# Retention and soft mixture of experts in one kernel: where block copies of y run, and which key tiles are loaded twice

## The chip, the cores and the metric

One core of a Trainium2 chip runs the whole kernel. The metric is device time in microseconds, from one launch; the times shown are medians over runs of the same program. Engines by their names in the profile: PE is TensorE's matmul side and PEld its weight loads, DVE is VectorE, ACT is ScalarE, POOL is GpSimd, SP is SyncE, which issues every DMA of this kernel.

## The reference

Two stages. The first is retention over 4 batches, 8 heads, 768 tokens, head size 64, with a decay `gamma` per head:

```
state = gamma * state + k_t (outer) v_t
y_t   = q_t @ state / sqrt(D)
```

The second takes y as x, 3072 tokens by 512, through a soft mixture of 8 experts with 4 slots each. All in float32:

```
logits = x @ phi                          # 3072 x 32
slot_input = softmax over tokens (logits).T @ x
slot_out[e] = relu(slot_input[e] @ w1[e]) @ w2[e]
out = softmax over slots (logits) @ slot_out
```

## The kernel before, in words

The tokens of a sequence are cut into chunks of 128, and one chunk of one batch is a step: 24 steps, two of them a pair, 12 pairs. The loop `for P in range(NPP)` (L505) makes one pass for each pair, numbered from 0 here as in the code: "pass 9" is the tenth. The order of all instructions on every engine is the order of the program text (`manual_schedule`, L96). Each pass does, for its pair:

- loads: `load_pair(P + 3)` (L229, for the last two pairs L223) and most times two weight blocks of 2 MB (`load_two`, L176). SyncE issues them in order and waits at each for its buffer; three buffers hold input pairs.
- GpSimd decays q and v of the next pair (L240, L245) and keeps the decay factors `qtab` going (L249).
- TensorE adds what the carried state gives (L280) and the values, scores times v (L289); ScalarE and VectorE copy the result out as y (L308, L309; in the last pass L305, L306). TensorE forms the state's increment from natural keys (L318), and VectorE adds it (L327).
- Keys come transposed from memory. Natural keys, needed at L318, are made by `turn_k`: four TensorE transposes (L234) and a ScalarE copy (L235), for the steps in `TURNED`. For the others (5, 7 and 9) a second, natural copy of the keys is loaded behind the pair's other inputs.
- y of a pair has to be turned to token order (`xn`) for the slot inputs. Either TensorE transposes it (`natural_mm`, L334) and ScalarE copies it out (`natural_copy`, L341); or, for the pairs in `MOVED`, one pass later VectorE turns all 32x32 blocks in place (`block_turn`, L345) into a tile `xb`, and 16 copies of 32 partitions by 256 elements put the blocks into order (`block_moves`, L355). `MOVES` says in which pass the copies run, in two parts of eight, and by which engine: a letter each, "s" for ScalarE, "g" for GpSimd, `MIX` five and three. 
- In every second pass the logits of four steps (L372), their exponentials on ScalarE (L395, L398, after VectorE's L402), and the slot sums of the four steps before (L428) follow. `combine_b` has one GpSimd operation (L474).
- At the end of a pass TensorE takes the scores of the next pair's two steps (L256), and VectorE masks them (L264) into a tile `A`.

Tiles `A`, y, `xb` and `xn` come from one ring of nine slots (`slot()`): a new tile takes a slot that has come back, and its first writer waits until that slot's last readers are done.

Behind the loop come the last slot inputs, the first expert layer (L671), the second (L757), taken in three blocks of output columns, and the combination (L733), whose pieces are copied out (L741) and stored (L744).

The constants that the change touches, L47 to L52:

```
TURNED = (0, 1, 2, 3, 4, 6, 8, 10, 11, 12, 13, 14, 15, 16, 17, 18, 19)
MOVED = (0, 2, 3, 4, 5, 6, 7, 8)
MIX = "sgssgssg"
MOVES = {1: [(0, 0, MIX)], 2: [(0, 1, MIX)], 9: [(8, 0, "s")], 10: [(8, 1, "g")]}
MOVES.update({P: [(P - 1, 0, MIX), (P - 1, 1, MIX)] for P in range(3, 9)})
```

The order in a pass, with lines left out:

```
        attend_copy(P)
        if P - 1 in MOVED:
            block_turn(P - 1)
...
        if P not in MOVED:
            natural_mm(P)
            natural_copy(P)
        for m in MOVES[P]:
            block_moves(*m)
```

Of the kernel before, what the change touches and what calls it, by code (L numbers as in the profile page):

```python
# [43 lines left out]
NIN = 3  # L44
NRING = 9
PACE = (0, 1, 0, 1, 1, 1, 1, 1, 1, 0, 1, 0)
TURNED = (0, 1, 2, 3, 4, 6, 8, 10, 11, 12, 13, 14, 15, 16, 17, 18, 19)  # L47
SIW = 48
MOVED = (0, 2, 3, 4, 5, 6, 7, 8)
MIX = "sgssgssg"  # L50
MOVES = {1: [(0, 0, MIX)], 2: [(0, 1, MIX)], 9: [(8, 0, "s")], 10: [(8, 1, "g")]}
MOVES.update({P: [(P - 1, 0, MIX), (P - 1, 1, MIX)] for P in range(3, 9)})  # L52
WITHK = [[i for i in (2 * P, 2 * P + 1) if i not in TURNED and i < NSTEP - B] for P in range(NPP)]
ROWS = [[P for P in range(1, NPP - B // 2) if len(WITHK[P]) == n] for n in range(3)]
KINDS = [n for n in range(3) if ROWS[n]]
# [31 lines left out]
def retention_soft_moe_kernel(  # L87
# [143 lines left out]
    def turn_k(i, name):  # L231
        kp = bank(name)
        for g in range(NPAIR):
            nc.tensor.transpose(kp[:, g * 128:(g + 1) * 128], st[i]["kT"][:, g, :], ident)  # L234
        nc.scalar.copy(st[i]["kn"], kp.rearrange("p (h d) -> p h d", d=D))  # L235
# [85 lines left out]
    def state_add(P):  # L321
        for k in range(2):
            d = sst[(2 * P + k) % B]
            if P < B // 2:
                nc.scalar.copy(d, pr[P]["S"][:, k])
            else:
                nc.vector.tensor_tensor(d, d, pr[P]["S"][:, k], ALU.add)  # L327

    def natural_mm(P, ks=(0, 1), names=("A2", "A3")):
        X = pr[P].setdefault("X", {})  # L330
        for k in ks:
            X[k] = bank(names[k])
            for g in range(NPAIR):
                nc.tensor.transpose(X[k][:, g * 128:(g + 1) * 128], pr[P]["yT"][:, k, g, :], ident)  # L334

    def natural_copy(P, engines=("scalar", "scalar"), ks=(0, 1)):
        if "xn" not in pr[P]:
            pr[P]["xn"] = slot()
        for k in ks:
            xn = st[2 * P + k]["xn"] = pr[P]["xn"][:, k * 512:(k + 1) * 512]  # L340
            (nc.scalar.copy if engines[k] == "scalar" else nc.vector.tensor_copy)(xn, pr[P]["X"][k])  # L341

    def block_turn(P):
        x = pr[P]["xb"] = slot()
        nc.vector.transpose(x, pr[P]["yT"].rearrange("p i g t -> p (i g t)"))  # L345

    def block_moves(P, part, on="sg"):
        if part == 0:
            xn = pr[P]["xn"] = slot()
            for k in range(2):  # L350
                st[2 * P + k]["xn"] = xn[:, k * 512:(k + 1) * 512]
        x = pr[P]["xb"].rearrange("p (m b d) -> p m b d", b=4, d=32)
        xn = pr[P]["xn"].rearrange("p (m a d) -> p m a d", a=4, d=32)
        for n, (a, b) in enumerate((a, b) for a in (2 * part, 2 * part + 1) for b in range(4)):
            {"s": nc.scalar.copy, "g": nc.gpsimd.tensor_copy}[on[n % len(on)]](xn[32 * b:32 * b + 32, :, a], x[32 * a:32 * a + 32, :, b])  # L355
# [149 lines left out]
    for P in range(NPP):  # L505
# [50 lines left out]
        if P < NPP - B // 2:  # L556
            state_mm(P)
            state_add(P)
        if P - 1 in MOVED:
            block_turn(P - 1)  # L560
        for k in range(2):
            if 2 * P + 2 + k in TURNED:
                turn_k(2 * P + 2 + k, ("A2", "Y0")[k] if P % 2 == 0 else f"A{k}")
        if P == NPP - 2:
            for m in MOVES[P]:
                block_moves(*m)
# [9 lines left out]
            continue  # L576
# [5 lines that stand above are left out]
# [255 lines left out]
```

## Time and profile before

| | us |
|---|---|
| median of 3 runs | 150.73 (150.56 to 150.92) |
| the profiled execution | 150.77 |
| its span, first to last instruction | 149.1 |
| PE busy | 138.0 (93%) |
| DVE busy | 89.2 (60%) |
| ACT busy | 70.1 (47%) |
| POOL busy | 68.1 (46%) |
| DMA moved | 60.06 MB, mean 403 GB/s |

Times of rows are microseconds from the span's start. A matmul of this kernel shows as two records. Busy time of PE counts overlapping matmuls once.

### The profile page before, as it was taken

Reading aid. Unit: us, or ns where it says so; the run is one execution under the profiler, and the core shown is the slowest. Engines: PE = TensorE matmul, PEld = TensorE weight load, DVE = VectorE, ACT = ScalarE, POOL = GpSimd, SP = SyncE. Lnnn points to the kernel's source line nnn. Section 1 sums busy time; section 2 is a strip of 40 time slices with the busy share of each in tenths; the row PEclk is TensorE's granted clock in tenths of the full one; section 3 lists DMA queues with packets and bytes.
Section 4 is the critical chain, followed back from the end, with each engine's and each line's share of the span. In section 5 each row is a group of like instructions: output and inputs, shape, how many; then the busy total and the mean of one; then the engine's idle time right before and its main releaser. Section 6 shows DMA issues by size and latency. Waiting matters only on the chain.

```text
span 149.1 us, 5532 instructions
## 1 busy us (share of the span) xinstructions
PE 138.0 (93%) x2382; PEld 102.3 (69%) x2382; DVE 89.2 (60%) x195; ACT 70.1 (47%) x172; POOL 68.1 (46%) x121
## 2 busy tenths in 40 slices
PE   7999999989999999999999999599999999999820
PEld 2778989877999799979996888465333365656600
DVE  0497837776887997799886883457510101564450
ACT  3123472737779766988587823141510000352240
POOL 1172497986969796796592989210200000000000
PEclk9999999999999999999999999999999999999997
DMA  4999999999999999999999999999999999799696
GB/s 138 408 446 411 445 428 426 420 400 440 425 425 418 398 442 414 439 402 435 420 431 418 431 418 426 415 425 404 403 442 422 422 426 431 308 400 411 276 383 247
DMA packets 6937, 60.06 MB, mean 403 GB/s; under 512 B 768, under 2 KB 768, under 8 KB 3712
## 3 DMA queue, kind: packets, MB, share of 16 engines
q1 hardware_dynamic: 6912, 59.70, 96.2%
q8 instruction: 19, 0.31, 0.8%
q14 instruction: 6, 0.05, 0.1%
HBM read 53.41 MB, written 6.29 MB: 400 GB/s over the span
## 4 chain that ended last, share of the span: by engine, by line
PE 61%; DMA 23%; POOL 6%; DVE 4%; issue 1%; SPq 1%; DVEq 0%; POOLq 0%
DMA b<-in_x_dram 10%; DMA b<-in_xw_dram 10%; PE A L757 10%; PE Y L289 8%; PE A L256 8%; PE Y L671 5%; PE A L671 5%; PE S L318 5%; PE Y L280 3%; DMA r<-in_head_dram 3%; PE sm L372 3%; PE A L234 2%; POOL r L355 2%; POOL b L245 2%; PE sm L733 2%; DVE b L741 2%
## 5 line engine op out<-in xcount | busy, mean ns | idle before, releaser
L264 DVE TENSOR_TENSOR r<-A,mi 128x512 f32<-128x512 f32 (+1 forms) x50 | 30.2, 662 | 16.3 <-PE A L256 13.4
L355 ACT COPY r<-r 32x256 f32<-32x256 f32 x78 | 31.4, 402 | 3.1 <-DVE r L345 2.2
L256 PE MATMUL A<-b 64*128 64x128 f32 x384 | 25.5, 280 | 0.3 <-DMA b<-in_kq_dram 0.3
L256 PEld LDWEIGHTS A<-b 64*128 64x128 f32 x384 | 22.7, 187 | 3.3 <-issue 1.8
L245 POOL TENSOR_TENSOR b<-b,kt 128x512 f32<-128x512 f32 x23 | 23.8, 1054 | 0.9 <-DMA b<-in_x_dram 0.9
L355 POOL COPY r<-r 32x256 f32<-32x256 f32 x50 | 19.8, 395 | 6.9 <-PE S L428 2.8
L289 PE MATMUL Y<-r,b 128*64 128x128 f32 x352 | 22.2, 277 | 0.3 <-POOL b L245 0.3
L289 PEld LDWEIGHTS Y<-r,b 128*64 128x64 f32 x352 | 19.2, 137 | 2.6 <-issue 1.2
L240 POOL TENSOR_TENSOR b<-b,qtab 128x256 f32<-128x256 f32 x20 | 14.3, 735 | 13.0 <-DMA b<-in_x_dram 9.2
L757 PE MATMUL A<-b,r 128*32 128x128 f32 (+1 forms) x352 | 14.4, 304 | 0.1
L757 PEld LDWEIGHTS A<-b,r 128*32 128x32 f32 x352 | 9.6, 109 | 6.2 <-issue 3.8
L741 ACT COPY b<-A 128x384 f32<-128x384 f32 x10 | 4.5, 483 | 17.0 <-PE A L733 15.3
L318 PE MATMUL S<-b 128*64 128x64 f32 x304 | 10.7, 222 | 0.0
L280 PE MATMUL Y<-b,sst 64*64 64x128 f32 x304 | 10.6, 276 | 0.0
L318 PEld LDWEIGHTS S<-b 128*64 128x64 f32 x304 | 10.3, 138 | 0.0
L345 DVE STREAM_TRANSPOSE r<-r 128x1024 f32<-128x1024 f32 x8 | 9.9, 1238 | 0.0
L280 PEld LDWEIGHTS Y<-b,sst 64*64 64x64 f32 x304 | 8.2, 132 | 1.2
L309 DVE TENSOR_TENSOR r<-Y,qtab 128x512 f32<-128x512 f32 x9 | 6.2, 692 | 4.6 <-PE Y L289 4.6
L235 ACT COPY b<-A 128x512 f32<-128x512 f32 x11 | 6.3, 588 | 5.7 <-PE A L234 2.3
L372 PEld LDWEIGHTS sm<-r,kt 128*32 128x32 f32 x192 | 5.4, 110 | 2.6 <-issue 2.4
L327 DVE TENSOR_TENSOR sst<-sst,S 128x256 f32<-128x256 f32 x16 | 6.0, 418 | 1.9 <-PE S L318 1.9
L671 PE MATMUL A<-b,qtab 128*32 128x512 f32 x64 | 7.1, 594 | 0.0
(160 smaller groups left out, 194.3 us busy)
## 6 DMA issues: line engine op xcount, KB each, us to landing
b<-in_wtwo_dram SPq DMA_DIRECT2D x12, 2048.0 KB, 17.2
b<-in_x_dram SPq DMA_DIRECT2D x5, 1536.0 KB, 12.7
b<-in_x_dram SPq DMA_DIRECT2D x3, 1792.0 KB, 11.1
b<-in_xw_dram SPq DMA_DIRECT2D x2, 2048.0 KB, 16.1
out_dram<-b SPq DMA_DIRECT2D x5, 768.0 KB, 5.6
b<-in_wl_dram SPq DMA_DIRECT2D x2, 1536.0 KB, 11.8
r<-in_whalf_dram SPq DMA_DIRECT2D x5, 512.0 KB, 12.3
out_dram<-b SPq DMA_DIRECT2D x6, 384.0 KB, 3.3
```

Of the source, the lines that this page charges most:

```text
L240: nc.gpsimd.tensor_tensor(q[:, 0:2], q[:, 0:2], qtab[:, 0:2], ALU.mult)
L245: nc.gpsimd.tensor_tensor(v, v, vsc[:, i // B, a:b].unsqueeze(2).broadcast_to([128, b - a, D]), ALU.mult)
L256: nc.tensor.matmul(s["sc"][r][:, g, :], s["kT"][half(r), g, :], s["qT"][half(r), g, :], start=True, stop=True, skip_group_check=True)
L264: nc.vector.tensor_tensor(s["A"][:, r, g:g + n], s["sc"][r][:, g:g + n], mask.unsqueeze(1).broadcast_to([128, n, C]), ALU.mult)
L280: nc.tensor.matmul(p["y"][k][b][half(half_of(r, g)), gl, :], sst[(2 * P + k) % B][half(r), g, :], s["qT"][half(r), g, :], start=(gl == 0 a ...
L289: nc.tensor.matmul(pr[P]["y"][k][g // 2][half(half_of(r, g)), g % 2, :], s["v"][:, 2 * g + r, :], s["A"][:, r, g, :], start=(P < B // 2 an ...
L318: nc.tensor.matmul(S_[half(r), k, g, :], s["kn"][:, 2 * g + r, :], s["v"][:, 2 * g + r, :], start=True, stop=True, skip_group_check=True)
L345: nc.vector.transpose(x, pr[P]["yT"].rearrange("p i g t -> p (i g t)"))
L355: {"s": nc.scalar.copy, "g": nc.gpsimd.tensor_copy}[on[n % len(on)]](xn[32 * b:32 * b + 32, :, a], x[32 * a:32 * a + 32, :, b])
L372: nc.tensor.matmul(q["ltp"][32 * j:32 * j + 32, :], phis[:, p, :], st[GRP * g + j]["yT"][:, p, :], start=(p == 0), stop=(p == NPAIR - 1), ...
L671: nc.tensor.matmul(hp[hf][32 * j:32 * j + 32, :], si0[:, a:a + NSLOT], w1t[hf, g, k][j], start=(g == 0 and k == 0), stop=(g == 1 and k == ...
L757: nc.tensor.matmul(op[32 * j:32 * j + 32, :w], hT[fc // 4][:, fc % 4, 4 * g + j, :], w2t[4 * g + j, cb, fc], start=(n == 0), stop=(n == le ...
```

## The change

Pair 1's y goes by block turn and copies in pass 2 instead of TensorE's transposes in pass 1, so pair 0's sixteen copies all run in pass 1. Pair 7's copies in pass 8 alternate between the two engines. Pair 8's copies all run in pass 9, fourteen on ScalarE and two on GpSimd, and pass 10 has none. Steps 7 and 9 get their natural keys by `turn_k`, in passes 2 and 3, and the loads of pairs 3 and 4 no longer hold them.

```diff
-TURNED = (0, 1, 2, 3, 4, 6, 8, 10, 11, 12, 13, 14, 15, 16, 17, 18, 19)
+TURNED = (0, 1, 2, 3, 4, 6, 7, 8, 9, 10, 11, 12, 13, 14, 15, 16, 17, 18, 19)
 SIW = 48
-MOVED = (0, 2, 3, 4, 5, 6, 7, 8)
+MOVED = (0, 1, 2, 3, 4, 5, 6, 7, 8)
 MIX = "sgssgssg"
-MOVES = {1: [(0, 0, MIX)], 2: [(0, 1, MIX)], 9: [(8, 0, "s")], 10: [(8, 1, "g")]}
-MOVES.update({P: [(P - 1, 0, MIX), (P - 1, 1, MIX)] for P in range(3, 9)})
+MOVES = {1: [(0, 0, MIX), (0, 1, MIX)], 2: [(1, 0, MIX), (1, 1, MIX)], 8: [(7, 0, "sg"), (7, 1, "sg")], 9: [(8, 0, "s"), (8, 1, "sssg")], 10: []}
+MOVES.update({P: [(P - 1, 0, MIX), (P - 1, 1, MIX)] for P in range(3, 8)})
```

## Rows read from the trace of the kernel before

**Rows 1.** Windows: busy us (instructions) by engine, PE clock, DMA share, GB/s

```profile
core 0: us, PE busy (x) PEld busy (x) DVE busy (x) ACT busy (x) POOL busy (x), PEclk, DMA share, GB/s
...
30.00:60.00 30.00, 29.58 (x584) 26.17 (x580) 24.73 (x53) 21.35 (x54) 24.25 (x42) 1.00 1.01 422
60.00:90.00 30.00, 29.64 (x581) 25.72 (x578) 25.28 (x54) 22.20 (x57) 21.79 (x38) 1.00 1.01 424
...
127.00:131.00 4.00, 4.00 (x84) 2.27 (x80) 2.14 (x5) 1.72 (x4) 0.00 (x0) 1.00 0.71 300
...
138.00:142.00 4.00, 3.59 (x70) 2.33 (x63) 1.62 (x5) 0.93 (x3) 0.00 (x0) 1.00 0.71 284
```

**Rows 2.** Chain of waits, 73 to 97 us: start, length, what

```profile
72.99 14.28 DMA b<-in_xw_dram
...
96.37 0.44 PE S L289 x7
```

**Rows 3.** Timeline, 88 to 104 us: start, length, engine, line, operation [idle before, releaser]

```profile
90.49 1.16 PE L256 MATMUL A<-b 64*128 64x128 f32 x16
...
90.88 3.46 POOL L355 COPY r<-r 32x256 f32<-32x256 f32 x8
...
92.62 1.09 PE L289 MATMUL Y<-r,b 128*64 128x128 f32 x16
...
94.38 1.29 DVE L264 TENSOR_TENSOR r<-A,mi 128x512 f32<-128x512 f32 x2 [2.89 <-POOL r L355]
...
95.12 0.43 PE L289 MATMUL A<-r,b 128*64 128x128 f32 x2 [1.41 <-DVE r L264]
```

**Rows 4.** Timeline, 81 to 89 us

```profile
81.90 3.31 ACT L355 COPY r<-r 32x256 f32<-32x256 f32 x8
...
82.36 1.43 POOL L240 TENSOR_TENSOR b<-b,qtab 128x256 f32<-128x256 f32 x2 [3.03 <-DMA b<-in_xw_dram]
...
83.15 1.86 PEld L256 LDWEIGHTS A<-b 64*128 64x128 f32 x32 [0.28 <-POOL b L240]
...
87.40 1.41 POOL L240 TENSOR_TENSOR b<-b,qtab 128x256 f32<-128x256 f32 x2 [0.68 <-DMA b<-in_xw_dram]
...
88.15 0.37 ACT L395 ACTIVATE pT<-sm,nmc 128x128 f32<-128x128 f32 x1 [2.95 <-DVE lq L402]
```

**Rows 5.** Timeline, 72 to 82 us

```profile
74.89 4.13 ACT L355 COPY r<-r 32x256 f32<-32x256 f32 x10 [0.34 <-DVE r L345]
...
80.18 1.09 PE L334 MATMUL A<-mi,r 128*128 128x128 f32 x8 [0.35 <-ACT r L308]
```

**Rows 6.** DMA issues: tiles, engine, count, KB each, median us to landing

```profile
b<-in_x_dram SPq DMA_DIRECT2D x3, 1792.0 KB, 11.1
...
out_dram<-b SPq DMA_DIRECT2D x5, 768.0 KB, 5.6
```

**Rows 7.** Chain of waits: transposes of pass 1, and a turn's second half

```profile
18.02 0.87 PE A L334 x8
...
41.79 0.44 PE Y L234 x4
```

**Rows 8.** Timeline, 19 to 36 us: TensorE in pass 3

```profile
33.42 1.06 PE L428 MATMUL S<-r,pl 128*32 128x512 f32 x8 [0.42 <-DVE sst L327]
```

**Rows 9.** Groups by form: the block turn | busy us, mean ns | idle before

```profile
L345 DVE STREAM_TRANSPOSE r<-r 128x1024 f32<-128x1024 f32 x8 | 9.9, 1238 | 0.0
```

**Rows 10.** Single DMA issues of L176 and L744: start, us to landing

```profile
L176 SPq DMA_DIRECT2D b<-in_wtwo_dram x1: 328/328/328, 109.4 to 109.4; - x1
...
DMA to landing us min/median/max: 17.4/17.4/17.4
...
L176 SPq DMA_DIRECT2D b<-in_wtwo_dram x1: 328/328/328, 111.1 to 111.1; - x1
...
DMA to landing us min/median/max: 22.1/22.1/22.1
...
L744 SPq DMA_DIRECT2D out_dram<-b x1: 351/351/351, 129.4 to 129.4; - x1
```

**Rows 11.** Timeline, 104 us to the end: TensorE in the last block

```profile
136.65 2.61 PE L757 MATMUL A<-b,r 128*32 128x128 f32 x88
```

## The prediction, made before the changed kernel was run

> **What bounds the kernel now.** I read the windows view first [rows 1]. From 30 to 90 us TensorE is busy 29.6 of every 30.0 us and the 16 DMA engines are busy throughout (share 1.01): two resources are full at once. The idle time lies elsewhere: the DMA engines are idle for 29% of the 4 us from 127 and of the 4 us from 138, 2.3 us in all, while outputs are not ready. So before 127 us the stream is full, and behind it the outputs, and with them TensorE's place in time, set the end.
>
> The chain of waits [rows 2] then tells where the loop's end hangs: on the last input pair, issued at 72.99 and landed 14.28 later at 87.27, on GpSimd behind it, and at last on the values of step 23, done at 96.81. The timeline of that stretch [rows 3] shows the place: GpSimd copies blocks for 3.46 us from 90.88. VectorE's mask of step 23 starts at 94.38 after 2.89 us of idle time, released by those copies: the mask takes a ring slot that they still read. TensorE has done the scores of step 23 at 91.65 (90.49 + 1.16), finishes the values of step 22 at 93.71 (92.62 + 1.09), stands 1.41 us, and takes the values of step 23 in pieces. Behind that point the chain is TensorE almost alone, so what is won here arrives at the end, if the outputs' transfers allow it.
>
> **The change part by part.** The sum is made against the profiled execution's 150.77 us (span 149.1, 1.7 around it), 0.04 over the median of the runs.
>
> *Block copies out of pass 10.* Eight GpSimd copies go (3.46 us, eight times 0.43 [rows 3]). In pass 9 ScalarE gets six more and GpSimd two. The mask of step 23 can then start when its scores are there, at about 91.7, and takes 1.3 us: done at 93.0, before TensorE needs it at 93.7. The values of step 23 take 1.09 us behind those of step 22, so they end at 94.8 instead of 96.8: 2.0 us. At least the 1.41 us of plain standing should come back if the slot is free; nothing comes back if the mask gets another late slot. I take 2.0, as every instruction on this path has its own row. Next in line is TensorE itself; the copies of the values behind it move along.
>
> *What pays for it in pass 9.* ScalarE's queue: eight copies from 81.90 (3.31 us) become fourteen, about 5.8 us at 0.41 each, ending at 87.7. Behind them wait the exponential at 88.15, which has 2.95 us of idle time before it [rows 4], the scale factor and the copies of pair 10's values, for which TensorE's transposes wait in turn. 2.5 of the 2.95 us are filled; cost 0, and 0.4 if everything else moves forward but the copies do not. GpSimd's queue: two copies (0.86 us) stand before the small product of the combine weights, the next decay factors and the decays of steps 22 and 23. Before those decays GpSimd stood 0.68 us for the landing [rows 4]; with the copies it is 0.18 late instead, unless all that it does in this pass starts earlier, with the input of step 20, which the part on the keys brings forward. Cost 0, bound 0.2.
>
> *Pass 8.* Pair 7's copies go from ten and six to eight and eight. ScalarE's ten take 4.13 us [rows 5]; two fewer give 0.83. There TensorE's transposes stood 0.35 us, released by a ScalarE copy that had queued behind these ten. That wait goes: 0.35, or nothing if another engine is as late. GpSimd's two more (0.86 us) fall into the 3.03 us in which it waits for the next input [rows 4]; cost 0, and if the input came over 2 us earlier they would delay the decays by the rest.
>
> *Keys of steps 7 and 9.* Each was 256 KB of a 1792 KB load [rows 6]: the loads of pairs 3 and 4 shrink to 1536 KB, 0.52 MB less, and SyncE issues the same loads in the same order. At 424 GB/s [rows 1] that is 1.24 us for every landing behind them, as the stream is full up to 127. It pays where TensorE waits for a landing: 0.28 us at the scores of step 20 [rows 4]; most of this I count, 0.2. For the rest TensorE is late by itself. The price is a turn by TensorE, 0.44 us for four transposes [rows 7], and a ScalarE copy each. Step 7's turn, in pass 2, is on the path: 0.44 lost. Step 9's, in pass 3, falls into the 0.42 us in which TensorE waits for VectorE's state add [rows 8]: 0, bound 0.44.
>
> *Pair 1 by block turn.* Eight TensorE transposes of pass 1 go, 0.87 us of the path [rows 7], and two ScalarE copies. VectorE gets one block turn, 1.24 us [rows 9], ahead of the masks of pass 2; ScalarE and GpSimd get ten and six copies in passes 1 and 2 each, where they had five and three. Pass 4, within 30 to 60 us, carries just this load already, and TensorE is busy 29.58 of those 30 us [rows 1], so I take 0 for the engines. GpSimd's decays come up to 1.3 us later in pass 2 (three copies more), and TensorE's values of step 6 would have to wait if that grew past their margin; bound 0.4. With step 7's turn: 0.87 - 0.44 = 0.43 won, bounds 0 and 0.87.
>
> *The end.* With the sum so far, 2.0 + 0.35 + 0.2 + 0.43 = 3.0 us, the outputs would be issued 3.0 us earlier, the weights land only 1.24 us earlier. The last weight tile was issued at 111.1 and landed 22.1 us later, at 133.2 [rows 10]. TensorE's last block runs from 136.65 with 88 matmul records in 2.61 us [rows 11], and the second half of its experts, which needs that tile, is the last 64 of them, so from about 137.4. That margin of 4.2 us shrinks by 3.0 - 1.24 to 2.4: no wait. The DMA engines have 2.3 us of holes to close beyond the 1.24, so 3.5 us is the most the stream lets go; some engines have smaller holes than the mean. I take 0.1 off (bounds 0 and 1.8, the latter if no hole closes). Sum: 2.9; 150.77 - 2.9 - 0.04 gives **147.8 us**.
>
> **A rule of the skill at this place.** The tile ahead of the last was issued at 109.4 and landed 17.4 later, at 126.8, so the last tile of equal size came 6.4 us behind it, where 2048 KB at 424 GB/s are 4.9; the first output had been issued at 129.4 [rows 10]. The Trainium skill (DMA: Bandwidth & Descriptors, Queues, rings and completion order) says that each engine takes the descriptors of one ring in their order, so that outputs queued behind weights cannot hold them up; by it the last tile lands 1.24 us earlier whatever the outputs do, and rival 4 below cannot happen. The trace agrees only in part, as the last tile took 1.5 us more than its bytes. The sum is 2.9 us either way: held back by 1.5, the tile would land at 132.0 and still be in time.
>
> **The rivals.**
> 1. *The stream sets the end.* TensorE comes earlier, but the holes of the outputs do not all close, as they may lie on other engines of the 16 than the ones that finish last. Then the gain is between 1.24 and about 2.2 us: 148.5 to 149.5. For: the DMA share of 1.01 up to 127. Against: the first hole ends where the first output is issued, and outputs 3.0 us earlier fall right into it.
> 2. *Only the mask's wait goes.* VectorE's masks or ScalarE's queue in pass 9 hold TensorE where it was, and pass 2 eats what pass 1 wins: 150.7 - 2.0 = 148.7.
> 3. *The change does not free the slot.* The ring hands out slots as they come back; one tile more is taken in pass 2, so the mask of step 23 could get one that is read later, by ScalarE's fourteen copies or by pair 10's work. At their end of 87.7 it would still be in time for 91.7; only a slot freed about 94 leaves the wait: 150.0 to 150.7. Against: the tile that held it is now read out a pass earlier.
> 4. *Slower: outputs push the last weights back.* Outputs now start at about 126.4, while the last tile is under way. Alone it would land at 126.8 - 1.2 + 4.9 = 130.5. If four outputs (768 KB [rows 6], 1.85 us each at 424 GB/s) all went ahead of it, it would land at 137.9, against a need at 137.4 - 3.0 = 134.4: TensorE waits 3.5 us, more than the 2.9 won, 151.3. It decides from 3.9 us of transfers that go first, and turns the sign at 6.8. For: the 6.4 us. Against: in the trace the outputs in flight cost it 1.5 at most.
>
> **How the numbers follow.** Forecast 0.58, rival 1 0.18, rival 2 0.10, rival 3 0.07, rival 4 0.07. A measurement of this kernel tells about 0.2%, 0.3 us, from no change. Faster: forecast, rivals 1 and 2 and a third of rival 3: 0.88. Same: the rest of rival 3, 0.05. Slower: rival 4, 0.07. The forecast's own range goes from 147.1 (3.5 us, all that the stream lets go, and 0.1 for the runs' spread) to 148.4 (2.0 for the mask and 0.3 of the 1.0 from the rest). Rivals 1 and 2 carry it to 149.4; rivals 3 and 4 and the uppermost part of rival 1 stay out, under 2 in 10.
>
> **What would show it.** Right: VectorE's masks of pass 10 wait for score matmuls, no longer for block copies; the values of step 23 follow those of step 22 without a gap; they end near 93.8; the landing of the last pair lies near 86.0; the DMA share is over 0.9 around 125 to 140. Wrong, if GpSimd or ScalarE still release that mask, if TensorE waits in pass 9 for ScalarE's copies, or if matmuls of the last block wait for a weight load.

## The result, and the profile after

The changed kernel takes 149.52 us (median of 4 runs, 149.31 to 149.71) where the kernel before took 150.82 beside it (4 runs, 150.56 to 151.26): a ratio of 0.9908, interval 0.9891 to 0.9924. It is faster by 1.3 us. The prediction said 147.8 us and a range up to 149.4: the sign was right, the size was not, and the time lies just outside the range, at the upper end of rival 1. The profiled execution took 149.71 us. Some executions of a program are slower as a whole; ratios here leave these out, so a ratio can rest on fewer runs than the count beside it.

The page of the changed kernel:

```profile
span 147.7 us, 5550 instructions
...
DMA packets 6936, 59.52 MB, mean 403 GB/s; under 512 B 768, under 2 KB 768, under 8 KB 3712
...
L264 DVE TENSOR_TENSOR r<-A,mi 128x512 f32<-128x512 f32 (+1 forms) x50 | 30.2, 662 | 11.9 <-PE A L256 11.9
...
b<-in_x_dram SPq DMA_DIRECT2D x7, 1536.0 KB, 11.9
...
out_dram<-b SPq DMA_DIRECT2D x5, 768.0 KB, 6.9
...
out_dram<-b SPq DMA_DIRECT2D x6, 384.0 KB, 4.2
```

VectorE's masks (L264) are no longer released by block copies. The loads of 1792 KB of [rows 6] are down to one. But an output of 768 KB now takes 6.9 us from issue to landing, where it took 5.6 [rows 6]. TensorE's side is seen in the timeline from 79 to 94 us (start, length, engine, line, operation, idle time before and releaser), which answers to [rows 3 to 5]:

```profile
78.98 1.09 PE L334 MATMUL A<-mi,r 128*128 128x128 f32 x8
...
81.12 5.79 ACT L355 COPY r<-r 32x256 f32<-32x256 f32 x14 [0.31 <-DVE r L345]
...
82.09 1.86 PEld L256 LDWEIGHTS A<-b 64*128 64x128 f32 x32 [0.42 <-POOL b L240]
...
84.79 0.84 POOL L355 COPY r<-r 32x256 f32<-32x256 f32 x2
...
86.64 1.42 POOL L240 TENSOR_TENSOR b<-b,qtab 128x256 f32<-128x256 f32 x2
...
87.09 0.37 ACT L395 ACTIVATE pT<-sm,nmc 128x128 f32<-128x128 f32 x1 [0.18 <-DVE lq L402]
...
87.42 0.97 PEld L256 LDWEIGHTS A<-b 64*128 64x128 f32 x16 [0.39 <-POOL b L240]
...
90.84 1.29 DVE L264 TENSOR_TENSOR r<-A,mi 128x512 f32<-128x512 f32 x2 [0.20 <-PE A L256]
...
91.77 1.09 PE L289 MATMUL Y<-r,b 128*64 128x128 f32 x16
...
92.70 0.60 PE L289 MATMUL A<-r,b 128*64 128x128 f32 x8
```

Step 23's mask starts at 90.84, 0.20 us after VectorE's last work and released by a score matmul; in [rows 3] it was 94.38 after 2.89 us. TensorE goes from the values of step 22 (91.77) straight into those of step 23 (92.70). The 0.35 us before the transposes at L334 [rows 5] are gone, and the exponential at L395 waits 0.18 us instead of 2.95 [rows 4]: ScalarE's queue is as full as worked out, and no fuller. The chain of waits (start, length, what) gives the places on the path:

```profile
24.91 0.59 PE A L234 x4
25.50 0.44 PE Y L234 x4
...
33.91 0.87 PE sm L372 x32
...
63.48 17.69 DMA b<-in_xw_dram
...
93.30 0.44 PE S L289 x8
...
95.21 0.39 issue
```

The values of step 23 end at 93.74 (93.30 + 0.44), 3.07 us earlier than the 96.81 of [rows 2]; the forecast place was 93.8. Then 0.39 us of plain issue stand in the chain, which a second profiled execution of this kernel (below) does not have.

So TensorE is where it was to be, and the time is not. The windows (columns as in [rows 1]) and single issues show the other side:

```profile
60.00:90.00 30.00, 29.71 (x572) 25.74 (x566) 25.55 (x53) 23.79 (x62) 23.55 (x40) 1.00 1.01 425
...
127.00:131.00 4.00, 4.00 (x80) 2.04 (x76) 2.19 (x5) 1.82 (x5) 0.00 (x0) 1.00 0.90 369
131.00:138.00 7.00, 6.83 (x164) 4.68 (x156) 2.94 (x8) 1.83 (x5) 0.00 (x0) 1.00 0.97 394
138.00:142.00 4.00, 1.95 (x18) 1.09 (x16) 2.92 (x7) 2.28 (x6) 0.00 (x0) 1.00 0.86 342
```

```profile
L176 SPq DMA_DIRECT2D b<-in_wtwo_dram x1: 327/327/327, 108.7 to 108.7; - x1
...
DMA to landing us min/median/max: 23.3/23.3/23.3
...
L744 SPq DMA_DIRECT2D out_dram<-b x1: 348/348/348, 127.0 to 127.0; - x1
...
DMA to landing us min/median/max: 6.9/6.9/6.9
...
L744 SPq DMA_DIRECT2D out_dram<-b x2: 655/854/1053, 141.1 to 141.8; - x2
...
DMA to landing us min/median/max: 4.8/4.9/5.0
```

Somewhat more than half of the holes of [rows 1] has closed: the share from 127 is 0.90 where it was 0.71, from 138 it is 0.86 where it was 0.71. The first output is issued 2.4 us earlier (127.02, before 129.41), the last 2.5 us earlier (141.83, before 144.36), but the last lands 5.0 us after its issue, before 3.9: of the 2.5 us, 1.1 are lost between issue and landing.

### The profile page after: what moved, and what is told of

Same layout as the page of the kernel before. It is cut to its first block, busy times and chain, and to the rows that moved or that the text cites. A ratio compares the mean times of both kernels' runs of the same rounds, so it can differ in the third digit from the quotient of the medians.

```text
span 147.7 us, 5550 instructions
## 1 busy us (share of the span) xinstructions
PE 137.8 (93%) x2382; PEld 102.3 (69%) x2382; DVE 90.6 (61%) x196; ACT 76.0 (51%) x186; POOL 68.9 (47%) x123
## 3 DMA queue, kind: packets, MB, share of 16 engines
HBM read 52.88 MB, written 6.29 MB: 401 GB/s over the span
## 4 chain that ended last, share of the span: by engine, by line
PE 70%; DMA 15%; POOL 5%; DVE 2%; issue 2%; SPq 1%; DVEq 0%; POOLq 0%
DMA b<-in_xw_dram 12%; PE A L256 11%; PE Y L289 10%; PE A L757 10%; PE S L318 5%; PE Y L671 5%; PE A L671 5%; PE Y L280 5%; DMA r<-in_head_dram 3%; PE A L234 3%; PE sm L372 3%; POOL b L245 2%; DVE b L741 2%; PE sm L733 2%; PE S L428 1%
## 5 line engine op out<-in xcount | busy, mean ns | idle before, releaser
L355 ACT COPY r<-r 32x256 f32<-32x256 f32 x92 | 37.0, 402 | 3.3 <-DVE r L345 2.0
L264 DVE TENSOR_TENSOR r<-A,mi 128x512 f32<-128x512 f32 (+1 forms) x50 | 30.2, 662 | 11.9 <-PE A L256 11.9
L256 PEld LDWEIGHTS A<-b 64*128 64x128 f32 x384 | 22.6, 187 | 3.8 <-issue 1.5
L355 POOL COPY r<-r 32x256 f32<-32x256 f32 x52 | 20.6, 396 | 4.6 <-PE S L428 1.4
L345 DVE STREAM_TRANSPOSE r<-r 128x1024 f32<-128x1024 f32 x9 | 11.1, 1237 | 0.0
L318 PE MATMUL S<-b 128*64 128x64 f32 x304 | 10.6, 222 | 0.0
L318 PEld LDWEIGHTS S<-b 128*64 128x64 f32 x304 | 10.2, 138 | 0.0
L235 ACT COPY b<-A 128x512 f32<-128x512 f32 x12 | 6.8, 588 | 4.5 <-PE A L234 4.1
L372 PEld LDWEIGHTS sm<-r,kt 128*32 128x32 f32 x192 | 5.4, 110 | 3.3 <-issue 3.3
L234 PE MATMUL A<-mi,b 128*128 128x128 f32 x48 | 7.2, 282 | 0.0
L474 POOL TENSOR_TENSOR cn<-cn,cz 128x128 f32<-128x128 f32 x6 | 2.4, 401 | 10.1 <-DVE cz L473 9.8
```

What stands on the lines that cost most here:

```text
L256: nc.tensor.matmul(s["sc"][r][:, g, :], s["kT"][half(r), g, :], s["qT"][half(r), g, :], start=True, stop=True, skip_group_check=True)
L264: nc.vector.tensor_tensor(s["A"][:, r, g:g + n], s["sc"][r][:, g:g + n], mask.unsqueeze(1).broadcast_to([128, n, C]), ALU.mult)
L318: nc.tensor.matmul(S_[half(r), k, g, :], s["kn"][:, 2 * g + r, :], s["v"][:, 2 * g + r, :], start=True, stop=True, skip_group_check=True)
```

## The experiments

Theory: TensorE comes about 3 us earlier as forecast, and the stream of transfers, which only got 0.52 MB shorter, sets the end. Rival: TensorE still sets it and lost its gain somewhere behind 94 us. Ratios are to the kernel before on the same chip, whose median was 150.98 there (150.88 in the last two runs).

**1. The moves alone** (loads as before):

```diff
-TURNED = (0, 1, 2, 3, 4, 6, 7, 8, 9, 10, ...
+TURNED = (0, 1, 2, 3, 4, 6, 8, 10, ...
```

> The changed kernel with the two key tiles loaded again (TURNED as before), so the full 0.52 MB more to move, and all moves of block copies as changed. Stream theory (the DMA engines have no idle time left until the last output has landed, so bytes set the end; before, the landings of the outputs had one gap of 0.6 us): only that gap can go, 150.1 to 150.6 us, though the values of step 23 end 2.5 to 3 us earlier than before. TensorE theory (the end follows TensorE, and the output phase only lost some time by chance): 148.0 to 148.8 us.

Measured 150.64 us (12 runs), ratio 0.9946, interval 0.9910 to 0.9982. TensorE's values of step 23 end at 95.24 (94.63 + 0.61), 1.6 us before [rows 2] and not 2.5 to 3 as expected, and of this 0.3 arrive at the end. The time lies at the upper edge of the stream's figure; with all of the 1.6 us it would have been 149.4.

**2. The turned keys alone** (the kernel before, with the new TURNED):

> The kernel before with the key tiles of steps 7 and 9 turned instead of loaded, and no other edit. Stream theory: the stream is 1.24 us shorter, but TensorE still stands for the mask, outputs are issued as late as before, and the end is theirs: 150.4 to 150.9 us. A theory in which bytes alone count, wherever TensorE is: 149.5 us. TensorE theory: 150.5 to 151.0 us (a turn of 0.44 us in pass 2, against 0.28 us of waiting for an input).

Measured 149.52 us (6 runs), ratio 0.9895, interval 0.9852 to 0.9939: as fast as the whole change. The timeline of this kernel:

```profile
93.07 1.29 DVE L264 TENSOR_TENSOR r<-A,mi 128x512 f32<-128x512 f32 x2 [1.33 <-POOL r L355]
...
94.85 0.65 PE L289 MATMUL S<-r,b 128*64 128x128 f32 x7
```

The mask still waits for GpSimd's copies, but they, the decays ahead of them and the landing ahead of those all come 1.3 us earlier, and the values end at 95.50 instead of 96.81. Neither theory's figure saw this: both took TensorE as hardly moved by the keys. The 149.5 on record for the bytes alone is met, but not quite for its reason: the last output lands 3.9 us after its issue, as before, so TensorE still sets this end, 1.3 us earlier. It takes the changed kernel's time because TensorE's end here, and in the kernel before, lies only 0.2 to 0.3 us behind what the stream allows (table under 7).

**3. The copies of pair 8 as before**, the rest of the change kept:

```diff
-9: [(8, 0, "s"), (8, 1, "sssg")], 10: []}
+9: [(8, 0, "s")], 10: [(8, 1, "g")]}
```

> The changed kernel with pair 8's copies back where they were (eight on ScalarE in pass 9, eight on GpSimd in pass 10), all else as changed. Both theories: the mask of step 23 waits for GpSimd again and TensorE's values of step 23 end about 2 us later than in the changed kernel. Stream theory: outputs have about 0.9 us of slack there, so the time is 150.4 to 150.8 us. TensorE theory: 2.0 us more than the changed kernel, 151.3 to 151.7 us.

```profile
93.13 1.29 DVE L264 TENSOR_TENSOR r<-A,mi 128x512 f32<-128x512 f32 x2 [2.75 <-POOL r L355]
...
93.88 0.43 PE L289 MATMUL A<-r,b 128*64 128x128 f32 x2 [1.27 <-DVE r L264]
```

Measured 149.79 us (7 runs), ratio 0.9915, interval 0.9876 to 0.9953. The whole stall is back, 2.75 us on VectorE and 1.27 on TensorE, as in [rows 3], and it costs 0.3 us or less against the changed kernel. Both figures on record were too high, the stream's by 0.6 to 1.0: the stall costs nearly nothing once the stream sets the end.

**4. A shorter stream**: the changed kernel without the load of the last weight tile of 2048 KB; the tile ahead of it is used in its place. The line that sets up `last_two` is left out here.

```diff
-        t = large(weight_pool[0])
-        nc.sync.dma_start(t, wtwo[n_two[0]])
+        if n_two[0] < 11:
+            t = large(weight_pool[0])
+            nc.sync.dma_start(t, wtwo[n_two[0]])
+            last_two[0] = t
+        t = last_two[0]
```

> The changed kernel without the load of the last 2 MB tile of second-layer weights; the tile ahead of it is used in its place, so the last block's second half of experts is computed with wrong weights, by the same instructions. Nobody waited for that tile. Stream theory: its 4.9 us go from the stream, outputs then follow TensorE as it stands in the changed kernel (its last output is issued 2.5 us earlier than before): 147.2 to 148.0 us. TensorE theory: no change, 149.4 to 149.7 us.

Measured 147.66 us (4 runs, 147.64 to 148.20), ratio 0.9785, interval 0.9741 to 0.9829. TensorE does the same work, and with 4.9 us out of the stream's way the program ends where the prediction saw TensorE alone end it, at 147.8. This is the run that tells the theory from its rival.

**5. TensorE later, by 0.9 and by 3 us**: more warming matmuls ahead of the weights' first block.

```diff
-    warm(1, "A0")
+    warm(3, "A0")
```

> The changed kernel with two more idle matmuls of 256 columns ahead of the first expert layer, 0.9 us more on TensorE's path. Stream theory: outputs have about that much slack, 149.4 to 149.8 us. TensorE theory: 150.3 to 150.5 us.

Measured 149.28 us (6 runs), ratio 0.9884, interval 0.9853 to 0.9915: nothing lost. Its first output is issued at 127.04, no later than the 127.02 above, whose execution had lost time in the issue gap; the run under 7 is the one to hold it against. With 8 instead of 3:

> The changed kernel with seven more such matmuls, 3.0 us more on TensorE's path. Stream theory: the slack of 0.9 to 1.3 us is used up first, 151.2 to 151.8 us. TensorE theory: 152.4 to 152.7 us.

Measured 151.31 us (10 runs), ratio 1.0014, interval 0.9979 to 1.0049. First output at 129.28, last output landing 3.9 us after its issue: of 3 us of delay 1.8 arrive (151.31 - 149.52), so the changed TensorE had a little over 1 us to give, as the theory has it.

**6. Less stream, by another turn.** Step 5's keys turned too, with its load cut, in two forms. The first changes TURNED alone:

```diff
+TURNED = tuple(range(20))
```

> The changed kernel with step 5's keys turned too, the last that were loaded twice: 0.26 MB less to move, and 0.44 us more for TensorE in pass 1. Stream theory: 0.6 us less, 148.8 to 149.1 us. TensorE theory: 149.5 to 150.0 us, no gain or a loss.

Measured 148.44 to 151.99 us (6 runs), ratio 0.9821, interval 0.9749 to 0.9892: spread too far to tell half a microsecond. The ratio rests on the two runs of 148.44 and 148.63; the other four took 151.18 and more. Run again:

> The kernel with the keys of all steps turned, timed once more, as few of its runs were undisturbed. Stream theory: 148.4 to 149.0 us. TensorE theory: 149.5 to 150.0 us.

149.24 us (6 runs, 148.57 to 152.94), ratio 0.9875, interval 0.9831 to 0.9918. Of these twelve runs five took 148.44 to 148.80, about the stream theory's figures and less than the fastest of the changed kernel's ten (149.31); the two profiled executions, 151.61 and 149.68, are not among them. The first loads landed late in both profiles, the head's released GpSimd at 7.80 and 7.74 instead of 6.84. The second form leaves the arrays as they are and cuts only what is loaded:

```diff
-            for a in ((0, 1536), (1536, 3072)) if P == 1 else ((0, 3072 + 512 * n),):
+            for a in ((0, 1536), (1536, 3072)) if P == 1 else ((0, 3072),):
...
-            if 2 * P + 2 + k in TURNED:
+            if 2 * P + 2 + k in TURNED or 2 * P + 2 + k == 5:
```

> The changed kernel with step 5's keys turned too, and its load cut to the 1536 KB that are used, but every array in memory left as it is in the changed kernel (in the run with all steps turned the arrays' sizes changed as well, and the first loads landed 0.9 us later). Stream theory, with the late first loads put down to the arrays: 148.5 to 149.0 us, and the first loads land as in the changed kernel. If the late first loads come from elsewhere: as the run with all steps turned, near 149.2 us, the first loads late again. TensorE theory: 149.5 to 150.0 us.

149.42 us (6 runs, 148.86 to 149.64), ratio 0.9880, interval 0.9846 to 0.9914, beside 149.61 for the changed kernel on the same chip. Its first loads landed nearly as in the changed kernel (GpSimd released at 6.96), and the gain expected with that did not come. Fewer bytes do not make it slower, but 0.2 us is less than the 0.5 to 1.0 expected, and the intervals overlap: whether it beats the changed kernel stays open.

**7. The changed kernel again:**

> The changed kernel itself, on the same chip as the run before it: 149.3 to 149.7 us by either theory.

149.61 us (6 runs, 149.39 to 150.50), ratio 0.9912, interval 0.9877 to 0.9946. Its profiled execution took 149.45 us and has no issue gap: the values of step 23 end at 93.63, the first output is issued at 126.23, 3.2 us before [rows 10]. It is the cleanest view of the end. Windows of this execution:

```profile
127.00:131.00 4.00, 3.94 (x89) 2.19 (x84) 2.75 (x6) 2.39 (x6) 0.00 (x0) 1.00 0.97 397
131.00:138.00 7.00, 6.48 (x148) 4.44 (x142) 2.94 (x9) 1.72 (x4) 0.00 (x0) 1.00 0.94 384
138.00:142.00 4.00, 1.57 (x16) 0.86 (x13) 2.13 (x5) 1.63 (x4) 0.00 (x0) 1.00 0.96 387
142.00:143.00 1.00, 0.00 (x0) 0.00 (x0) 0.00 (x0) 0.00 (x0) 0.00 (x0) 1.00 1.02 406
143.00:144.00 1.00, 0.00 (x0) 0.00 (x0) 0.00 (x0) 0.00 (x0) 0.00 (x0) 1.00 1.02 412
144.00:145.00 1.00, 0.00 (x0) 0.00 (x0) 0.00 (x0) 0.00 (x0) 0.00 (x0) 0.55 0.56 224
145.00:146.00 1.00, 0.00 (x0) 0.00 (x0) 0.00 (x0) 0.00 (x0) 0.00 (x0) 0.50 0.13 52
146.00:147.00 1.00, 0.00 (x0) 0.00 (x0) 0.00 (x0) 0.00 (x0) 0.00 (x0) 0.50 0.02 6
```

The same last stretch of the kernel before:

```profile
145.00:146.00 1.00, 0.00 (x0) 0.00 (x0) 0.00 (x0) 0.00 (x0) 0.00 (x0) 1.00 1.02 399
146.00:147.00 1.00, 0.00 (x0) 0.00 (x0) 0.00 (x0) 0.00 (x0) 0.00 (x0) 0.94 1.00 396
147.00:148.00 1.00, 0.00 (x0) 0.00 (x0) 0.00 (x0) 0.00 (x0) 0.00 (x0) 0.50 0.67 261
```

Before, all 16 DMA engines work to 147 and stop together within the next microsecond. In the changed kernel the holes are nearly closed (0.97, 0.94, 0.96), but the engines do not stop together: the share is 0.56 from 144, and 0.13 from 145, which is two engines of 16 (0.13 x 16 = 2.1), and those two set the end. From 142 the shares add up to 2.75 us of work for each engine (1.02 + 1.02 + 0.56 + 0.13 + 0.02); shared out evenly it would be done at 144.75, some 1.5 us before the last engine.

**All runs on one line of reasoning.** From the first output's issue to the end of the program, by the profiled executions:

```
run                        first output  time     difference  last output,      last weight tile's
                                                              issue to landing  to last output's landing
kernel before              129.41        150.77   21.4        3.9               15.0
2  keys alone              128.10        149.45   21.4        3.9               15.0
4  shorter stream          126.36        147.66   21.3        3.9               -
5  3 us later              129.28        151.02   21.7        3.9               17.9
3  copies as before        128.16        150.00   21.8        3.9               15.3
5  0.9 us later            127.04        149.25   22.2        4.9               14.8
changed kernel             127.02        149.71   22.7        5.0               14.8
1  moves alone             127.83        150.65   22.8        4.9               14.7
7  changed kernel again    126.23        149.45   23.2        4.8               14.7
```

Where TensorE sets the end, the rest takes 21.3 to 21.8 us and the last output lands 3.9 us after its issue. Where it comes too early for the stream, the difference grows and the last landing takes 4.8 to 5.0. The last column shows the stream's side: the outputs' 6.29 MB take 14.8 us at the 424 GB/s of [rows 1], and in the runs that the stream holds the last output lands just that, 14.7 to 14.8 us, behind the last weight tile. In the kernel before it was 15.0: TensorE set its end, but by no more than 0.2 to 0.3 us. The earliest that the stream lets go is about 149.3 to 149.7 with the 0.52 MB gone and 150.6 with them (run 1), about 1 us apart, and 1.24 us is what these bytes take. The two forms of run 6 stand at 21.9 and 22.6. On this sum TensorE in run 7 would have ended the program at 126.23 + 21.4 = 147.6.

## Why the prediction was wrong, point by point

**The step that failed is "The end".** It took 0.1 us off, on the ground that the DMA engines' mean had 2.3 us of holes to close beyond the 1.24 us of bytes. Measured on run 7 it was 1.8 us (149.45 - 147.6), its outer bound. The mean was the wrong quantity: outputs issued earlier fill idle time on engines that are done with the weights, but the end is set by the engines that have most left to do, and on those there was 0.2 to 0.3 us to fill, not 2.3. The trace of the kernel before already shows it, in the landings of the first, the fifth and the last output:

```profile
L744 SPq DMA_DIRECT2D out_dram<-b x1: 351/351/351, 129.4 to 129.4; - x1
...
DMA to landing us min/median/max: 5.6/5.6/5.6
...
L744 SPq DMA_DIRECT2D out_dram<-b x1: 332/332/332, 137.8 to 137.8; - x1
...
DMA to landing us min/median/max: 4.4/4.4/4.4
...
L744 SPq DMA_DIRECT2D out_dram<-b x2: 805/847/889, 143.4 to 144.4; - x2
...
DMA to landing us min/median/max: 3.9/3.9/3.9
```

The last weight tile landed at 133.20 [rows 10], the first five outputs at 134.98, 136.70, 138.53, 140.36 and 142.18: 1.72 to 1.83 us apart, no more than the 1.85 that 768 KB take at 424 GB/s. The last landed at 148.24. So the engine that landed last had hardly a gap between outputs, and the whole stretch was 0.2 us longer than the 14.8 of its bytes. By this count the changed kernel's last output would land at 133.20 - 1.24 + 14.8 = 146.8, and with the 2.5 us from there to the end of the program (150.77 - 148.24) it would take 149.3.

The engines of a full stream are not in step: the trace's packet records give each engine's last write of a tile, and for the tile ahead of the last the first engine writes it at 121.77, the last at 125.12 in the changed kernel, 3.35 us apart. The text named this mechanism, as rival 1 and in "some engines have smaller holes than the mean", and gave it 0.18 where the forecast had 0.58. Its argument against, that the earlier outputs fall right into the first hole, is true of the mean (0.71 became 0.97 in run 7) and beside the point. The forecast's own sum with that bound, 150.77 - 3.0 + 1.8 - 0.04, gives 149.5. The signs that the text named for being right came all the same: the masks wait for score matmuls, the values of step 23 follow without a gap and end at 93.74, the last pair lands at 86.06, and only the share from 138 (0.86) is under 0.9. None of them looks at the engine that lands last.

**Block copies out of pass 10: right on TensorE.** 2.0 us were counted. The values of step 22 start at 91.77, 0.85 earlier than in [rows 3], those of step 23 end 3.07 earlier: 2.2 from the mask's stall. ScalarE's fourteen copies took 5.79 us (5.8 was worked out) and end at 86.91. At the end of the program it was worth 0.3 us or less (run 3).

**Pass 8 and pass 9: right, at the bound.** The wait at L334 went. In pass 9 TensorE waits 0.14 us longer at the scores of step 20 (0.42, before 0.28 [rows 4]), where it is now early for the landing, and 0.22 us longer at those of step 22 (0.39, before 0.17): there GpSimd's decays start at 86.64, 0.58 after their input has landed, as its two block copies stand ahead of them. From the one to the other TensorE's lead shrinks from 1.06 to 0.85 us, which is the 0.2 that the text gave as its bound.

**Pair 1 and step 7: right.** In the chain, L372 of pass 3 stands at 33.91, 0.57 before its old place of 34.48; 0.43 was forecast. Step 9's turn cost nothing: it fell into the wait of [rows 8], and L428 starts 1.03 us after the end of the state's increment at L318 (31.89 to 32.92), where it was 1.00 (32.42 to 33.42).

**Keys of steps 7 and 9: mis-sized.** 0.2 us were counted for the landings; by itself the part is worth 1.3 us on TensorE (run 2: 96.81 to 95.50). The wait for a landing that shows, 0.28 us, was only the one in front of TensorE. In [rows 2] the mask's stall itself hangs on the last landing, through GpSimd: the landing moved by the bytes' 1.2 us (87.27 to 86.06 in the changed kernel), and everything behind it followed. In the whole change this was partly counted already, as the mask's 2.0 us, so TensorE's sum came out right (3.07 for 3.0): moves alone 1.6 and keys alone 1.3 make 2.9. At the end it is what nearly the whole gain comes from.

**Rivals 2, 3 and 4 did not happen.** The slot was free, and TensorE's other gains arrived. Outputs issued up to 3.2 us earlier did not push the last weight tile back: it landed at 132.0 and in run 7 at 131.8 (107.9 + 23.9), 1.2 and 1.4 before its old 133.2, which is what the bytes give. The Trainium skill (DMA: Bandwidth & Descriptors, Queues, rings and completion order) says that each engine consumes the descriptors of one ring in their order; the traces agree, as far as these landings show it. That the tile came 6.4 us behind the tile ahead, here and in [rows 10], the text took to speak for rival 4. But one engine of the 16 alone was late with it; the others had it 4.9 us behind the tile ahead, as its bytes give (last section).

## What to carry to other kernels

Where a stream of transfers is full up to the last stage, a gain on the compute engine is worth only what the stream gives back, so a change that shortens both is worth the smaller of the two gains, and each part tried alone can look worthless or like the whole. A mean share of the DMA engines does not say how much of a hole can be closed, since the engine with most left to do sets the end. Look at the landings of the last transfers instead: if they follow each other as closely as their bytes allow, issuing them earlier wins nothing. And a landing early in a chain of waits is worth what hangs on the whole chain, not the idle time that it shows in front of one engine.

## What the runs showed of the hardware that was not expected

Two of the 16 DMA engines finish last in every profile of the changed kernel that the stream holds. The semaphore of a landing counts 16 increments in the trace, taken here as one for each engine. Of the last output's, fourteen come by 145.64 in the first profile and two at 146.41 and 146.85 (run 7: 145.34, then 146.42 and 146.58); in the kernel before all 16 come within 0.25 us. What the two have more to do is, by its times, the loading of instruction code, which takes place on the same engines:

```profile
q8 instruction: 18, 0.29, 0.8%
```

These are 18 packets of 16 KB, about 1.07 us each. In the first profile one runs from 128.79 to 129.88, and the data packet that starts at 129.87 takes 1.09 us instead of 0.61: 1.57 us together (run 7: a code packet at 127.93, then 1.10). Of the last weight tile's increments fifteen come by 130.47 and one at 132.01, 1.54 later. A second code packet, 0.94 us from 136.27, stands ahead of the fourth output, of which fourteen increments come by 137.86 and two at 139.02 and 139.39. In the kernel before, a code packet of 1.07 us from 131.05 goes with a last weight tile of which fifteen increments come by 131.63, 4.9 us behind the tile ahead (126.75), and one at 133.20. There, where TensorE holds the last outputs back, the late engine has caught up by the end; in the changed kernel it stays behind. In the run with 3 us of delay the packet comes at 129.87, the tile's 16 increments all come by 130.46, and it is the first output that one engine brings late (133.70, the others by 132.58). The records do not name a packet's engine, so the match is by times, and no run changed the code packets alone: that they are the cause is likely, not shown.

SyncE's issue of an output takes 0.33 to 0.35 us for most, but longer for some of the last, 0.88 us each for the last two of run 7. That is no sign that the stream is behind: the kernel before has 0.77, 0.81 and 0.89 among its last five, and run 4 has 0.84 for its last. What sets it stays open. In run 7 the last output was so issued at 141.8 although its last copy had ended at 140.67 (140.12 + 0.55), 1.1 us before; in the kernel before it was 0.5:

```profile
L744 SPq DMA_DIRECT2D out_dram<-b x2: 343/348/352, 126.2 to 127.9; - x2
...
L744 SPq DMA_DIRECT2D out_dram<-b x2: 881/884/887, 140.8 to 141.8; - x2
```

So an output issued late is no proof that the engine ahead of it was late.
